# Moving the filling no-operations on TensorE in a fused retention and feed-forward kernel

## The chip, the core and the metric

The kernel runs on one core of a Trainium2 chip. The metric is the device time of one execution in microseconds (us). The engines of the core are named as in the profile: PE is TensorE (matmuls), PEld its weight loads, DVE is VectorE, ACT is ScalarE, POOL is GpSimd, SP is SyncE, which issues most transfers. Each engine has a sequencer that takes the engine's instructions from a stream in order. A no-operation is an instruction that only the sequencer handles.

## The reference

Retention over 8 batches, 8 heads, 576 positions and a head size of 64, and then a feed-forward layer with a squared ReLU over all 4608 tokens:

```python
scores = (q @ k.transpose(0, 1, 3, 2)) / np.sqrt(64)
gamma = 1.0 - 2.0 ** (-5.0 - np.arange(8))
rel = pos[:, None] - pos[None, :]
Dmat = np.where(rel >= 0, gamma[:, None, None] ** rel, 0.0)
attn = (scores * Dmat) @ v                      # [8, 8, 576, 64]
x = attn.transpose(0, 2, 1, 3).reshape(4608, 512)
r = np.maximum(x @ w_in, 0.0)                   # w_in: 512 x 2048
out = (r * r) @ w_out                           # w_out: 2048 x 512
```

All inputs and the output are float32; the kernel multiplies in float16 and sums in float32.

## The kernel before

The 4608 tokens are cut into 36 units of 128, and these into 18 groups of two. For each group the kernel loads q, k and v, casts them to float16 and brings q and k into transposed form (for the first eight units by matmuls with an identity, line 581, output psT; copies at line 598 make kqT of it). The retention of a group is made of small matmuls on quarters of the 128 x 128 array. They are all issued by one helper, at line 499: scores (psc), sums of the running state (psS) and outputs (psO). From group 4 on, the outputs of one group and the scores and sums of the next are issued as one task, a long run of 96 to 128 small matmuls, each with its own weight load, so of 194 to 258 instructions. Two TensorE instructions stand for each matmul in the stream, a weight load and the matmul.

The feed-forward layer takes x of a group (xT) through w_in (line 1226, output ph), ReLU and square on ScalarE and VectorE, and w_out (line 1267 for group 0, line 1324 after that, output po). From group 1 on, the second product is done by Strassen's scheme with seven products of half the size in place of eight (sums gS on VectorE, line 1297). Groups 13 to 16 do the first product in the same way (line 1069). Before the change and after it this is the same.

The program is written out by a planner, `Schedule`. A kernel's piece of work is a task with an engine, a modelled duration `dur`, tasks that it depends on, and a `size`, roughly its number of TensorE instructions. `emit` plays the tasks through a model of the engines, with a key for each task from the table PLACES, and so gets one order for all of them. Then it calls `place_runs` with TensorE's tasks in this order. `place_runs` writes into tasks a number `pad`; and when the program is at last written out, each task's instructions are followed by `pad` no-operations on TensorE (`sched.filler`, line 393). No other engine gets any.

Warm-up matmuls (line 408, 34 of them, tasks with keys of 10^6 at first and `size=2`) multiply zeros at the start. The first 15 have a modelled duration of 0.43 us, the very first one of 1.75.

In the kernel before, `place_runs` counts instructions and gives each long run (`size` over 200) a place within blocks of 256 instructions: where the run's place isn't between 60 and 196 behind an assumed edge, it spreads as many no-operations as bring it to 130 over the tasks since the last task of a size over 20. Three runs get some: 136, 125 and 128, in all 389.

Of the kernel before, what the change touches and what calls it, by code (L numbers as in the profile page):

```python
# [78 lines left out]
class Schedule:  # L79
# [118 lines left out]
            for i in range(t["pad"]):  # L198
                self.filler()

    BLOCK, EDGE, AHEAD_OF, SAFE = 256, 194, 130, (60, 196)

    def place_runs(self, tasks):

        at = 3
        between = []
        for t in tasks:
            if t["size"] > 200:
                phase = (at - self.EDGE) % self.BLOCK
                if not self.SAFE[0] <= phase <= self.SAFE[1]:  # L210
                    n = (self.AHEAD_OF - phase) % self.BLOCK
                    for i, x in enumerate(between):
                        x["pad"] += n * (i + 1) // len(between) - n * i // len(between)
                    at += n
            at += t["size"]
            if t["size"] > 20:
                between = []
            else:
                between.append(t)


# [1246 lines left out]
```

## Time and profile before

| what | value |
|---|---|
| three runs | 285.14, 285.28, 286.89 us |
| median | 285.28 us |
| profiled execution | 285.75 us |
| its span, first to last instruction | 284.0 us |
| instructions in the profile, all engines | 10,985 |
| no-operations at line 393 | 389 |
| granted TensorE clock, mean of the span | 1.000 |
| bytes moved | 50.00 MB, 176 GB/s on average |

A row of a timeline gives the start in us from the span's start, the length, the engine, the line, the operation, output and inputs by the program's names, the shape and the count; in brackets the idle time before and what ended it. A matmul's modelled length covers its way through the pipeline, so that rows overlap; the distance of two starts tells what one costs. A row of the chain of work that ended last gives start, length and what the time was spent on; "issue" in it is time in which an engine waited for nothing that the profile shows.

### The profile page before, as it was taken

The numbers are of one execution on the slowest core, as the hardware profiler recorded it, in microseconds if no ns is written. First come the engines' busy times: TensorE is split into PE (matmuls) and PEld (weight loads), VectorE is DVE, ScalarE is ACT, GpSimd is POOL, SyncE is SP. The second block draws the span as 40 slices with busy tenths as digits, with TensorE's granted clock in tenths as the row PEclk, the third lists the DMA queues.
The fourth block names the chain that finished last, engine by engine and source line by source line (L and its number), as shares of the span: only waits on it lengthen the run. The fifth ranks groups of instructions, "written<-read, shape, count | busy, mean of one in ns | idle before, by whom it ended". The sixth has DMA issues, their size and how long they took to land.

```text
span 284.0 us, 10985 instructions
## 1 busy us (share of the span) xinstructions
PE 277.2 (98%) x4538; PEld 236.1 (83%) x4538; DVE 196.3 (69%) x380; ACT 191.8 (68%) x357; POOL 85.4 (30%) x123
## 2 busy tenths in 40 slices
PE   8899999999999999999999999999999999999994
PEld 3577767887888888888888888898899999999983
DVE  4783589755777856746648668687798799874562
ACT  5659984678485856885577685757739585867830
POOL 6650036424334441524342523425141500000000
PEclk9999999999999999999999999999999999999999
DMA  7999999989799899999889888979997921120114
GB/s 211 288 207 207 263 312 239 178 224 162 175 193 211 161 218 193 199 248 193 202 210 213 191 175 198 163 171 223 172 208 177 179 95 39 39 76 2 39 38 148
DMA packets 119152, 50.00 MB, mean 176 GB/s; under 512 B 94784, under 2 KB 113728, under 8 KB 119104
## 3 DMA queue, kind: packets, MB, share of 16 engines
q1 hardware_dynamic: 114560, 44.84, 71.5%
q0 software_dynamic: 4224, 4.19, 8.9%
q8 instruction: 37, 0.61, 0.9%
q10 hardware_dynamic: 320, 0.26, 0.4%
q14 instruction: 11, 0.09, 0.1%
HBM read 36.70 MB, written 9.44 MB: 162 GB/s over the span
## 4 chain that ended last, share of the span: by engine, by line
PE 93%; POOL 2%; issue 2%; DVE 1%; ACT 1%; POOLq 0%; DVEq 0%
PE po L1324 37%; PE ph L1226 33%; PE ph L1069 9%; PE psO L499 5%; PE po L1267 2%; PE psS L499 2%; PE psc L499 2%; PE warm L408 1%; PE psT L581 1%; DVE gS L1297 1%; POOL mask L348 1%; ACT rl L1234 0%; POOL vx L559 0%; POOL w_in L475 0%; DVE o L1347 0%
## 5 line engine op out<-in xcount | busy, mean ns | idle before, releaser
L1226 PE MATMUL ph<-xT,w_in 128*128 128x256 f16 x896 | 108.0, 273 | 0.0
L1226 PEld LDWEIGHTS <-w_in 128*128 128x128 f16 x896 | 86.5, 98 | 11.8 <-issue 0.5
L1234 ACT ACTIVATE rl<-ph 128x512 f16<-128x512 f32 x112 | 65.5, 589 | 27.3 <-PE ph L1226 26.3
L1244 ACT ACTIVATE gT<-rl 128x512 f16<-128x512 f16 x94 | 59.0, 630 | 2.5
L1324 PEld LDWEIGHTS <-gS 128*128 128x128 f16 x544 | 51.3, 98 | 7.3 <-issue 0.6
L1324 PE MATMUL po<-wT,gS 128*128 128x256 f16 x408 | 55.2, 273 | 0.1
L1324 PEld LDWEIGHTS <-gT 128*128 128x128 f16 x408 | 38.6, 98 | 5.7 <-issue 0.6
L1324 PE MATMUL po<-w_out,gT 128*128 128x256 f16 x272 | 37.4, 273 | 0.0
L1297 DVE TENSOR_TENSOR gS<-gT,gS 128x512 f16<-128x512 f16 (+1 forms) x51 | 31.0, 614 | 9.3 <-ACT gT L1244 8.7
L529 POOL TENSOR_TENSOR v<-loads,vdec_full 128x512 f16<-128x512 f32 x24 | 27.0, 1125 | 29.1 <-DMA loads<-in_v_dram 13.9
L513 POOL CAST kq<-loads 128x512 f16<-128x512 f32 x32 | 21.8, 682 | 35.0 <-DMA loads<-in_k_dram 26.0
L1297 DVE TENSOR_TENSOR gS<-gT 128x1024 f16<-128x1024 f16 x34 | 27.0, 796 | 6.9 <-ACT gT L1244 5.8
L524 POOL CAST kq<-loads 128x512 f16<-128x512 f32 x24 | 15.6, 649 | 43.7 <-DMA loads<-in_q_dram 43.5
L1347 DVE TENSOR_TENSOR o<-po,u 128x256 f32<-128x256 f32 x33 | 13.9, 421 | 20.2 <-PE po L1324 15.8
L1337 ACT COPY u<-po 128x256 f32<-128x256 f32 x34 | 12.6, 370 | 18.9 <-PE po L1324 18.9
L895 DVE TENSOR_TENSOR xT<-psO,gam_full 128x512 f16<-128x512 f32 x28 | 18.5, 684 | 6.0 <-PE psO L499 5.9
L1103 DVE CUSTOM_DVE_ANT_0 gT<-ph,loads 128x512 f16<-128x512 f32 x24 | 16.0, 687 | 6.2 <-PE ph L1069 4.0
L1082 ACT COPY loads<-ph 128x512 f32<-128x512 f32 x24 | 13.7, 586 | 9.4 <-PE ph L1069 8.9
L1324 PE MATMUL po<-wT,gT 128*128 128x256 f16 x136 | 19.3, 273 | 0.0
L1324 PE MATMUL po<-w_out,gS 128*128 128x256 f16 x136 | 18.2, 273 | 0.0
L1117 ACT ACTIVATE gT<-gT 128x1024 f16<-128x1024 f16 x16 | 16.4, 1054 | 0.3
L835 DVE TENSOR_TENSOR rT<-psc,mask_full 128x512 f16<-128x512 f32 x24 | 16.0, 682 | 0.7 <-PE psc L499 0.7
(101 smaller groups left out, 324.8 us busy)
## 6 DMA issues: line engine op xcount, KB each, us to landing
out_dram<-o SPq DMA_DIRECT2D x32, 256.0 KB, 2.9
loads<-in_k_dram SPq DMA_DIRECT2D x24, 256.0 KB, 4.6
loads<-in_q_dram SPq DMA_DIRECT2D x96, 64.0 KB, 3.6
loads<-in_v_dram SPq DMA_DIRECT2D x24, 256.0 KB, 3.4
w_in<-in_moe_w_in_dram POOLq DMA_DIRECT2D x4, 512.0 KB, 9.1
w_out<-in_moe_w_out_dram POOLq DMA_DIRECT2D x4, 512.0 KB, 14.3
pair_c<-in_k_dram SPq DMA_DIRECT2D x2, 512.0 KB, 5.6
pair_c<-in_q_dram SPq DMA_DIRECT2D x4, 256.0 KB, 5.8
```

The costliest lines, as they stand in the source:

```text
L499: t = nc.tensor.matmul(out_, lhsT=lhsT, rhs=rhs, start=start, stop=True, skip_group_check=True, tile_position=(64 * row, 64 * col))
L513: op(out=out_.rearrange("p (n b a d) -> p n b a d", n=2, b=2, a=2), in_=in_.rearrange("p (a n b) d -> p n b a d", n=2, a=2))
L529: nc.gpsimd.tensor_tensor(out=t, in0=tile_of["v32", u], in1=vdec[kind].rearrange("p (h o) -> p h o", o=1).to_broadcast([P, H, D]), op=ALU. ...
L835: tile_of["masking", g] = nc.vector.tensor_tensor(out=tile_of["rT", g][:, :, a], in0=tile_of["psc", g][a].rearrange("p (s n i) -> p s n i" ...
L895: nc.vector.tensor_tensor(out=tile_of["x", g].rearrange("p n (s e i) -> p e (n s) i", s=n, e=2)[:, c], in0=y.rearrange("p (o t r) -> p o r ...
L1069: nc.tensor.matmul(out_[:, e], lhsT=left[:, m, fi * P:(fi + 1) * P], rhs=right()[:, m], start=fresh and e == 0 and m == 0, stop=m == HK - ...
L1117: nc.scalar.activation(out=t, in_=t, func=ACTF.Square)
L1226: nc.tensor.matmul(tile_of["ph", g, fb][:, j, :], lhsT=w_in16[:, m, fi * P:(fi + 1) * P], rhs=tile_of["x", g][:, m, :], start=(m == 0), st ...
L1234: nc.scalar.activation(out=t, in_=tile_of["ph", g, fb], func=ACTF.Relu)
L1244: nc.scalar.activation(out=t, in_=rl, func=ACTF.Square)
L1297: (nc.gpsimd if eng == "POOL" else nc.vector).tensor_tensor(out=tile_of["S", g][:, k, sl], in0=in0(sl), in1=in1(sl), op=op)
L1324: nc.tensor.matmul(tile_of["pb", g, bank], lhsT=left(i), rhs=right[:, i, :], start=(start and i == 0), stop=(i == HF - 1), skip_group_chec ...
```

## The change

`place_runs` no longer counts places in blocks. It takes the number of no-operations for each place from a list. The first number, 139, goes to the first 15 warm-up matmuls. The others go ahead of the runs of a `size` over 190, in order, over the tasks of `size` up to 8 that begin later than 24 us in the planner's model and stand since the last such run. Within a place they are spread in proportion to the tasks' modelled durations. The order of the tasks, and so of every other instruction, stays as it was.

```diff
-    BLOCK, EDGE, AHEAD_OF, SAFE = 256, 194, 130, (60, 196)
+    WARM, PADS = 15, (139, 34, 22, 4, 2, 66, 56, 44, 62, 2, 2, 10, 66)
 
     def place_runs(self, tasks):
 
-        at = 3
+        def spread(n, among):
+            total = sum(x["dur"] for x in among)
+            until, done = 0.0, 0
+            for x in among:
+                until += x["dur"]
+                upto = int(n * until / total + 1e-6)
+                x["pad"] += upto - done
+                done = upto
+
+        pads = iter(self.PADS)
+        spread(next(pads), [t for t in tasks if t["key"] >= 10 ** 6 and t["size"] == 2][:self.WARM])
         between = []
         for t in tasks:
-            if t["size"] > 200:
-                phase = (at - self.EDGE) % self.BLOCK
-                if not self.SAFE[0] <= phase <= self.SAFE[1]:
-                    n = (self.AHEAD_OF - phase) % self.BLOCK
-                    for i, x in enumerate(between):
-                        x["pad"] += n * (i + 1) // len(between) - n * i // len(between)
-                    at += n
-            at += t["size"]
-            if t["size"] > 20:
+            if t["size"] > 190:
+                spread(next(pads, 0), between or [t])
                 between = []
-            else:
+            elif t["size"] <= 8 and t["key"] < 10 ** 6 and t["start"] > 24.0:
                 between.append(t)
```

In the written program TensorE's stream grows from 9,505 to 9,625 instructions, no-operations from 389 to 509: 31 behind the first warm-up matmul, 7 or 8 behind each of the next 14, and 370 in the twelve other places.

## The prediction

> **What bounds the kernel now.** I read the first part of the page, then the chain that ended last, then TensorE's timeline, and last the records of the no-operations. Of the page:
>
> ```profile
> PE 277.2 (98%) x4538; PEld 236.1 (83%) x4538; DVE 196.3 (69%) x380; ACT 191.8 (68%) x357; POOL 85.4 (30%) x123
> PE 93%; POOL 2%; issue 2%; DVE 1%; ACT 1%; POOLq 0%; DVEq 0%
> q8 instruction: 37, 0.61, 0.9%
> ```
>
> TensorE works through 98% of the span and is 93% of the chain, so whatever makes its stream longer makes the kernel longer. The third line counts the packets of 16,384 bytes (0.61 MB in 37) that bring TensorE's own instructions; 256 instructions of 64 bytes fill one, and 37 of them make 9,472 of the stream's 9,505. No packet lies before 14.6 us.
>
> The start, from TensorE's timeline (start, length, line, operation, output and inputs, count, idle time before and its releaser):
>
> ```profile
> 5.07 0.98 PE L408 MATMUL warm<-wT 128*128 128x512 f16 x3
> 5.88 0.74 PE L581 MATMUL psT<-ident,kx 128*128 128x128 f16 x8
> 6.46 0.81 PE L408 MATMUL warm<-wT 128*128 128x512 f16 x3
> 7.10 0.71 PE L581 MATMUL psT<-ident,qx 128*128 128x128 f16 x8
> 7.65 1.46 PE L408 MATMUL warm<-wT 128*128 128x512 f16 x6
> 9.73 0.64 PE L499 MATMUL psc<-kqT 64*64 64x128 f16 x31 [0.46 <-DVE kqT L598]
> 10.70 0.45 PE L499 MATMUL psS<-vx,kx 64*64 64x64 f16 x32 [0.33 <-POOL vx L559]
> 16.51 0.70 PE L499 MATMUL psS<-vx,kx 64*64 64x64 f16 x32
> ```
>
> From 10.70 us on, TensorE hardly waits again. Until then GpSimd's vx (ready at 10.65) sets the pace, and TensorE's two idle spells (0.46 and 0.33) are all the slack that it has there.
>
> The no-operations cost TensorE's sequencer time. Between 66.8 and 68.06 us, by the view of line 393:
>
> ```profile
> L393 PEldq NOP  x16: 13/13/13, 66.8 to 68.0; - x16
> ```
>
> Their records start 71 ns apart (66.835, 66.905, 66.976, 67.047), and the same 1.26 us holds eight matmuls of 109 ns, 0.87 us of work. So four no-operations to two matmuls take some 0.315 us instead of 0.218. At most 1.26/16 = 79 ns go to one, pairs of weight load and matmul included; a pair by itself issues in about 20 ns. In the chain (start, length, what):
>
> ```profile
> 65.65 2.50 PE po L1324 x20
> 70.98 1.10 PE po L1324 x8
> 129.81 2.40 PE po L1324 x22
> 223.33 0.29 issue
> ```
>
> 20 x 109 ns is 2.18, 8 x 109 ns is 0.87: dense no-operations cost 0.32 and 0.23 us here. The 22 matmuls at 129.81 have about one no-operation each and take just 22 x 109 ns: at one each they are free. The "issue" at 223.33 is idle time that nothing in the profile ended.
>
> **The change part by part.** The order of TensorE's other 9,116 instructions and their waits stay; so do the instructions of all other engines and every DMA. 389 no-operations leave three places (136 among 96 matmuls before the run of small matmuls at 72.97, 125 among 166 before 132.14, 128 among 96 before 157.71). 509 come: 139 among the first 15 warm-up matmuls (31 behind the first, 7 or 8 behind each other), 370 over the twelve stretches from 24 us on.
>
> Step 1, warm-ups, to the first transposes. 12 warm-ups precede the transposes of kx, and 115 no-operations stand among these. 115 x 71 ns + 12 x 20 ns = 8.4 us from the first matmul at 1.25, so the transposes start at 9.7 instead of 5.88. They have no slack: the timeline shows no idle time before them, and VectorE's two casts of kx run from 5.13 to 6.16. A cold warm-up takes 0.43 us (nine in 1.25 to 5.07), less than 8 x 71 = 0.57, so TensorE itself hides none of the excess; without the 0.43 the price would be the same, as the sequencer is the later of the two.
>
> Step 2, from there to psS. Three more warm-ups with 24 no-operations: 24 x 71 + 3 x 20 ns = 1.8 us, so qx is transposed from 11.6 (7.10 before) to 12.2. The copies to kqT then take ScalarE and VectorE 0.6 to 0.7 us, until 12.95; six warm-ups (1.29 us, no no-operation among them) end later, at 13.4. psc's 32 matmuls (0.57 us in their second run) follow, and psS starts at about 14.1 instead of 10.70, with vx long there: **+3.4 us**. With 79 ns for a no-operation it is +4.5; for the lower end I let the slack swallow 0.4 more, +3.0. Behind psS nothing gives this back: GpSimd's w_in transfers wait for a load, not for TensorE, and the next casts sit on ScalarE with 0.8 us or more to spare.
>
> Step 3, dense no-operations removed. The chain's pieces with four to a pair of matmuls lose 0.32 (65.65), 0.09 (68.15), 0.05 (69.54), 0.08 (70.46), 0.23 (70.98), 0.09 (72.08) and 0.08 (155.90): **-0.94 us**; -0.7 to -1.1 by how the 109 ns is rounded. What replaces them is at most 66 among 166 or 62 among 116 matmuls, 0.4 to 0.55 each, and the 125 among 166 were free: cost nothing, hidden beside 109 ns matmuls. Were that cover gone, 62 would cost 4.4 us; no row suggests it.
>
> Step 4, waits for instructions. Counting TensorE's stream, its instruction 451 (195 + 256) stands in the psS at 16.51, which took 0.70 where its twin at 10.70 took 0.45; instruction 7,875 (195 + 30 x 256) stands at the gap at 223.33. So blocks begin at 195 + 256n, and both stalls are a block not yet there. The second: block edge 7,619 was passed 0.25 us into the run of small matmuls at 219.60, the packet for the block after next came at 221.32, took 0.93, and work went on at 223.6, 3.7 us behind the passing. Afterwards 7,619 lies 60 instructions ahead of that run, which are 25 matmuls or 2.7 us, and the next edge 196 into it, 1 us: 3.7 us, plus what the sequencer is ahead of TensorE (packets that start up to 1.7 us before their edge is executed show such a lead). The stall should vanish: -0.45 (the gap in matmul starts is 0.51 against 0.056). Edge 451 falls in the later psO, 6.3 us behind edge 195; the first packet needed 6.0 the last time: -0.24. Together **-0.69**, between -0.69 and +0.5 if a stall of this size appears elsewhere; I take -0.69, as the shortest other distance of two edges is 4.35 us. Small pauses inside the runs (0.07 to 0.2 us, some 0.8 in all) have edges inside the same runs as before: 0, from -0.4 to +0.4.
>
> [...]
>
> **Sum.** The profiled execution took 285.75 us: span 284.0 and 1.75 around it. 285.75 + 3.4 - 0.94 - 0.69 = 287.5. The median shown is 285.28, 0.47 below that execution, so on its scale the forecast is **287.0 us**, +0.6%. Its own range, from 3.0 and the full gains (1.1 + 0.69 + 0.4) to 4.5 and the small ones (0.7 - 0.5 - 0.4): 286.1 to 290.0 at the extremes (0.4 of the small pauses in both), 286.4 to 288.0 in the main.
>
> **Rivals.**
>
> The no-operations are hidden (faster): if one costs under about 40 ns at the start, 115 fit into the 4.6 us before 5.88, and only steps 3 and 4 remain: 285.28 - 1.63 = 283.65. For it: warm-ups have the sequencer idle 0.4 us each. Against it: the 71 ns stand in the records without exception, and are no shorter where the sequencer had nothing else to do.
>
> The clock opens late (slower still). The page's granted clock is full in every slice, but warm-up matmuls of 512 columns stand 427 ns apart until about 5.4 us, 4.1 after the first, and 216 ns apart from there: the array gets its full rate only then. After the change it is idle for 1.8 us behind the first matmul, then busy 0.43 in each 0.53 to 0.59 us. If the clock stays at half to psS, three warm-ups and eight transposes take 2.1 instead of 1.8 us (+0.3), the second transposes 0.4 more, six warm-ups 2.6 instead of 1.3, psc some 0.3 more: +2.3, 289.3. [...] The rows show it opening after 4.1 us of unbroken work, and nothing with less; I think that 75% will mostly do.
>
> The stalls do not go (the change doesn't do what it says): step 4 gives 0 or +0.5, and the sum is 287.7 to 288.2.
>
> **How the numbers follow.** Forecast 0.64, late clock 0.18, stalls stay 0.08, hidden 0.10. The range is 284.8 to 289.6: it leaves out the hidden case and the far ends of the late clock and of the forecast. A measurement of this kernel tells about 1% from no change: slower by more (over 288.13) is the late clock, half of the stalls and the top of the forecast, 0.28; faster by more (under 282.43) is beyond even the hidden case, 0.04; within 1%, 0.68.
>
> **What would show it.** kx's transposes at 9.7 and psS at 14.1 us (steps 1, 2); everything from there 3.2 us late; 20 matmuls in 2.18 us where 65.65 stands (3); no "issue" piece near the feed-forward matmuls behind the run at 219.60 (4); the clock's rise by the length of a warm-up matmul. I am wrong if the no-operations at the start lie closer than 71 ns, or if a later wait of TensorE shrinks by what the start lost.

## The result, and the profile after

| | before | after |
|---|---|---|
| median of 22 runs each, us | 286.16 (285.14 to 290.52) | 287.80 (286.60 to 289.44) |
| profiled execution, us | 285.75 | 288.55 |
| its span, us | 284.0 | 286.8 |

The ratio after to before is 1.0046, with a 95% interval of 1.0026 to 1.0067. The changed kernel is a little slower, by an amount that lies below the 1% that a measurement of this kernel tells from no change with few runs, and that 22 runs on each side resolve. It is the ratio of the means, 287.80 and 286.47 us, without the one slow execution of the kernel before, 290.52 us; by the medians the difference is 1.64 us, by these means 1.33. The forecast was 287.0 us, +0.6%.

Lines have moved by 4: 408 is 412 now, 581 is 585, 499 is 503, 1324 is 1328, 393 is 397. The first part of the page, the chain's shares and the instruction packets, for the changed kernel:

```profile
PE 279.0 (97%) x4538; PEld 237.5 (83%) x4538; DVE 195.3 (68%) x380; ACT 191.6 (67%) x357; POOL 87.5 (31%) x123
PE 97%; issue 1%; DVE 1%; DVEq 0%
q8 instruction: 37, 0.61, 0.9%
```

TensorE still sets the end. GpSimd has gone from the chain: before, the chain's first microseconds ran through GpSimd and its vx; now TensorE itself is late there. The start, from TensorE's timeline of the changed kernel (start, length, engine, line, operation, output and inputs, shape, count, idle time before and its releaser):

```profile
1.25 0.61 PE L412 MATMUL warm<-wT 128*128 128x512 f16 x1 [1.25 <-DVE wT L293]
3.54 6.39 PE L412 MATMUL warm<-wT 128*128 128x512 f16 x11 [1.68 <-issue]
9.87 1.01 PE L585 MATMUL psT<-ident,kx 128*128 128x128 f16 x8
10.68 1.49 PE L412 MATMUL warm<-wT 128*128 128x512 f16 x3
11.96 1.06 PE L585 MATMUL psT<-ident,qx 128*128 128x128 f16 x8
12.81 1.86 PE L412 MATMUL warm<-wT 128*128 128x512 f16 x6
15.07 0.42 PE L503 MATMUL psS<-vx,kx 64*64 64x64 f16 x32
20.86 0.44 PE L503 MATMUL psS<-vx,kx 64*64 64x64 f16 x32
```

The 31 no-operations behind the first warm-up matmul are the pause of 1.68 us. The transposes of kx start at 9.87, where they stood at 5.88, and psS at 15.07 instead of 10.70. The second psS takes 0.44 us, where it took 0.70: the wait inside it is gone. The lengths tell one thing more. Before, three warm-ups took 0.98 us in the row at 5.07 and 0.81 in the one at 6.46, and eight transposes 0.74; here they take 1.49 and 1.01, and the six warm-ups 1.86 instead of 1.46. Where no no-operations stand between them, a warm-up stands 427 ns from the next until 13.6 us, and 216 ns from there on. 216 ns is the array's full rate here, and it came only at 13.6 us, 8.2 later than before (5.4). The page's row of granted clock has a 9 (90% or more) in every slice here as before, so what sets the moment isn't shown; where the recorded texts say that the clock opens, the traces show this step from 427 to 216 ns.

Further on, pieces of the chain (start, length, what; 20 matmuls of 109 ns are 2.18 us, 8 are 0.87):

```profile
69.71 2.18 PE po L1328 x20
74.51 0.87 PE po L1328 x8
133.40 2.40 PE po L1328 x22
223.66 0.46 issue
```

The dense no-operations have gone: 2.18 us where 2.50 stood at 65.65, 0.87 where 1.10 stood at 70.98. But an "issue" piece still stands behind the run at 219.60 of before (now at 222.6). It has moved from the feed-forward matmuls into the run of small ones, and the distance of matmul starts there is 0.65 us too long. In TensorE's stream it is the same place as before, instruction 7,875.

The time can be booked by comparing the start of each matmul with the start of the same matmul before. The same booking was made for three more executions of the unaltered changed kernel (they come up again below):

| how much later than before (us), at | after | 1st again | 2nd again | 3rd again | forecast |
|---|---|---|---|---|---|
| psS (10.70 before) | 4.37 | 3.79 | 4.08 | 4.01 | 3.4 |
| behind the stall at 451 (16.93) | 4.11 | 3.57 | 3.86 | 3.80 | 3.16 |
| behind the dense stretch (72.01) | 3.21 | 2.85 | 2.96 | 2.90 | 2.30 |
| 199.69 | 2.98 | 2.65 | 2.21 | 1.94 | 2.22 |
| behind instruction 7,875 (223.62) | 2.89 | 2.02 | 2.01 | 1.53 | 1.77 |

The last row is what is left at the end. Its mean is 2.11 us, and 285.75 + 2.11 is 287.86, the median of the 22 runs within 0.1. The profiled execution of the table is the latest of the four.

### The profile page after: what moved, and what is told of

Same layout as the page of the kernel before. It is cut to its first block, busy times and chain, and to the rows that moved or that the text cites. A ratio compares the mean times of both kernels' runs of the same rounds, so it can differ in the third digit from the quotient of the medians.

```text
span 286.8 us, 11105 instructions
## 1 busy us (share of the span) xinstructions
PE 279.0 (97%) x4538; PEld 237.5 (83%) x4538; DVE 195.3 (68%) x380; ACT 191.6 (67%) x357; POOL 87.5 (31%) x123
## 4 chain that ended last, share of the span: by engine, by line
PE 97%; issue 1%; DVE 1%; DVEq 0%
PE po L1328 37%; PE ph L1230 34%; PE ph L1073 9%; PE psO L503 5%; PE warm L412 5%; PE po L1271 2%; PE psc L503 2%; PE psS L503 2%; PE psT L585 2%; DVE o L1351 0%; DVE p L1380 0%; DVE wT L293 0%; DVEq L1351 0%
## 5 line engine op out<-in xcount | busy, mean ns | idle before, releaser
L517 POOL CAST kq<-loads 128x512 f16<-128x512 f32 x32 | 21.2, 661 | 35.9 <-DMA loads<-in_k_dram 25.9
L1301 DVE TENSOR_TENSOR gS<-gT 128x1024 f16<-128x1024 f16 x34 | 24.1, 710 | 8.9 <-ACT gT L1248 7.8
L528 POOL CAST kq<-loads 128x512 f16<-128x512 f32 x24 | 16.8, 701 | 33.0 <-DMA loads<-in_q_dram 32.9
L1341 ACT COPY u<-po 128x256 f32<-128x256 f32 x34 | 12.6, 370 | 18.5 <-PE po L1328 18.5
L1250 DVE TENSOR_TENSOR gT<-rl 128x512 f16<-128x512 f16 x18 | 9.7, 541 | 14.2 <-ACT rl L1238 14.0
L412 PE MATMUL warm<-wT 128*128 128x512 f16 x34 | 14.1, 490 | 3.0 <-issue 1.7
```

The source lines that it names most:

```text
L412: nc.tensor.matmul(warm_ps[0], lhsT=junk[:, 0:P], rhs=junk, start=True, stop=True)
L517: op(out=out_.rearrange("p (n b a d) -> p n b a d", n=2, b=2, a=2), in_=in_.rearrange("p (a n b) d -> p n b a d", n=2, a=2))
L528: nc.gpsimd.tensor_copy(out=tile_of["kq", u][:, 1].rearrange("p (t a d) -> p a t d", t=4, a=2), in_=tile_of["q32", u].rearrange("p (a t) d ...
L1301: (nc.gpsimd if eng == "POOL" else nc.vector).tensor_tensor(out=tile_of["S", g][:, k, sl], in0=in0(sl), in1=in1(sl), op=op)
```

## The experiments

**No no-operations among the warm-ups.** The 139 move to the next place (34 + 139 = 173), so that every later instruction keeps its number in the stream.

```diff
-    WARM, PADS = 15, (139, 34, 22, 4, 2, 66, 56, 44, 62, 2, 2, 10, 66)
+    WARM, PADS = 15, (0, 173, 22, 4, 2, 66, 56, 44, 62, 2, 2, 10, 66)
```

> The changed kernel without any no-operation among the warm-up matmuls: the 139 go to the next place instead (173 in place of 34, among 258 matmuls from 24 us on), so that every long run keeps its instruction numbers. Theory of the sequencer's time: the transposes of kx are back at 5.9 us and psS at 10.7 (15.1 in the changed kernel), the 0.24 us stall of instruction 451 comes back, and 173 among 258 matmuls cost nothing: 4.1 us less than the changed kernel, about 283.7 where that has 287.8 and the kernel before 286.2. Rival, that the no-operations at the start are free or are paid back later and the changed kernel is slower for another reason (stalls at other block edges): no difference from the changed kernel, 287.8.

Measured: 284.13 us (8 runs) against 285.82 for the kernel before (13 runs on the same chip), ratio 0.9944 (0.9926 to 0.9963). From its timeline:

```profile
1.26 4.75 PE L412 MATMUL warm<-wT 128*128 128x512 f16 x12 [1.26 <-DVE wT L293]
5.84 0.61 PE L585 MATMUL psT<-ident,kx 128*128 128x128 f16 x8
10.76 0.45 PE L503 MATMUL psS<-vx,kx 64*64 64x64 f16 x32 [0.32 <-POOL vx L563]
16.57 0.38 PE L503 MATMUL psS<-vx,kx 64*64 64x64 f16 x22
17.18 0.28 PE L503 MATMUL psS<-vx,kx 64*64 64x64 f16 x10 [0.24 <-issue]
```

The start is that of the kernel before again: transposes at 5.84, psS at 10.76 behind vx, and the stall at instruction 451 is back. The 173 no-operations ahead of the first long run cost nothing that shows (the 20 matmuls behind 65.86 take 2.18 us). So what is slow in the change is the 139 at the start, and the other 370 make the kernel faster than before. Its profile also has a pause of 0.46 us at instruction 5,315, and none at 7,875.

**The no-operations at the start alone.** The kernel before, with its first 136 no-operations moved from the stretch ahead of the first long run to the first 15 warm-ups; the other two places stay.

```diff
+        first = next(i for i, t in enumerate(tasks) if t["size"] > 200)
+        n = sum(t["pad"] for t in tasks[:first])
+        for t in tasks[:first]:
+            t["pad"] = 0
+        among = [t for t in tasks if t["key"] >= 10 ** 6 and t["size"] == 2][:15]
+        total = sum(x["dur"] for x in among)
+        until, done = 0.0, 0
+        for x in among:
+            until += x["dur"]
+            upto = int(n * until / total + 1e-6)
+            x["pad"] += upto - done
+            done = upto
```

> The kernel before with one part of the change alone: its first 136 no-operations leave the 96 matmuls ahead of the run at 72.97 us and stand among the first 15 warm-up matmuls. Theory of the sequencer's time: psS at about 15 us instead of 10.70 (+4.3), instruction 451 no longer stalls (-0.24), and the dense stretch gives back 0.9: about +3.2, 289.4 where the kernel before has 286.2. Rival, no-operations at the start are free: only the 0.9 and 0.24 remain, 285.0.

Measured: 287.70 us (4 runs), ratio 1.0074 (1.0054 to 1.0093). From its timeline:

```profile
3.47 6.21 PE L420 MATMUL warm<-wT 128*128 128x512 f16 x11 [1.61 <-issue]
9.75 0.61 PE L593 MATMUL psT<-ident,kx 128*128 128x128 f16 x8
11.53 0.61 PE L593 MATMUL psT<-ident,qx 128*128 128x128 f16 x8 [0.24 <-issue]
11.98 1.46 PE L420 MATMUL warm<-wT 128*128 128x512 f16 x6
13.96 0.46 PE L511 MATMUL psS<-vx,kx 64*64 64x64 f16 x32
```

psS is 3.26 us late, the stall at 451 gives back 0.22 and the dense stretch 0.87; 2.18 us are left at 72.01 of before, and 1.96 at the end. That the start costs nothing is refuted (285.0 was its time). The 289.4 expected, with a late full rate in it, was too high: the full rate came at 9.5 us, ahead of the transposes, eight of which take 0.61 us. The stall at 7,875 stands in this kernel too, 0.90 us by the matmuls' starts, where the kernel before had 0.45 with the same stream behind 73 us: such a stall isn't the same in two executions.

**A denser array under the same no-operations.** Each of the first 15 warm-ups issues its matmul twice, so that the array is busy while the sequencer passes the no-operations. This adds 15 matmuls of zeros whose result nobody reads; 30 no-operations are taken from the next place to keep the later places in the stream.

```diff
-    WARM, PADS = 15, (139, 34, 22, 4, 2, 66, 56, 44, 62, 2, 2, 10, 66)
+    WARM, PADS = 15, (139, 4, 22, 4, 2, 66, 56, 44, 62, 2, 2, 10, 66)
...
-        nc.tensor.matmul(warm_ps[0], lhsT=junk[:, 0:P], rhs=junk, start=True, stop=True)
+        made.append(1)
+        for i in range(2 if len(made) <= 15 else 1):
+            nc.tensor.matmul(warm_ps[0], lhsT=junk[:, 0:P], rhs=junk, start=True, stop=True)
```

> The changed kernel with two matmuls in place of one in each of the first 15 warm-ups, so that the array stays busy between the no-operations (30 no-operations fewer in the next place keep the long runs' instruction numbers). Theory that the thinned warm-up opened the clock late (13.6 us in the changed kernel, 5.4 before): it opens before 9 us, the 24 no-operations ahead of the transposes of qx set the pace and psS comes at 14.1 instead of 15.07: 0.9 less, about 286.9 where the changed kernel has 287.8. Rival, that the clock opens when it will whatever stands there: 13.6 again, psS at 15.1 or a little later, 287.8 or 0.3 more.

Measured: 287.39 us (6 runs), ratio 1.0052 (1.0033 to 1.0071). From its timeline:

```profile
3.54 6.58 PE L414 MATMUL warm<-wT 128*128 128x512 f16 x22 [1.25 <-issue]
9.96 0.61 PE L588 MATMUL psT<-ident,kx 128*128 128x128 f16 x8
14.30 0.46 PE L506 MATMUL psS<-vx,kx 64*64 64x64 f16 x32
```

The full rate came at 6.97 us, and the transposes take 0.61 us where the changed kernel's first ones take 1.01. psS stands at 14.30, +3.6 with a full rate that comes ahead of the transposes; 3.4 was forecast for the no-operations alone, and three more warm-ups stand ahead of qx's transposes here. (Its profiled execution is the shortest of the six, 286.46 us: 3.6 us behind the kernel before at psS, and 0.77 at the end.) In the times, a gain of 0.4 to 0.8 us over the changed kernel can't be seen (ratios 1.0052 and 1.0046 to the kernel before, with intervals of 0.2% on each side). So the start's cost is chiefly the sequencer's, and the late full rate is a part that only the profile shows.

**Half of them.** 70 among the warm-ups, and the other 69 in the next place.

```diff
-    WARM, PADS = 15, (139, 34, 22, 4, 2, 66, 56, 44, 62, 2, 2, 10, 66)
+    WARM, PADS = 15, (70, 103, 22, 4, 2, 66, 56, 44, 62, 2, 2, 10, 66)
```

> The changed kernel with 70 no-operations among the first 15 warm-ups in place of 139 (15 behind the first, 3 or 4 behind each other), 69 more in the next place, so that the long runs keep their instruction numbers. Theory of the sequencer's time: 4 x 71 + 20 ns = 0.30 us is less than the 0.43 us of a warm-up at the half clock, so only the 15 behind the first delay TensorE (0.7 us), and the slack of 0.8 us ahead of psS takes that: psS within 0.5 us of 10.7, the time that of the kernel with none there (284.1) to 0.5 more. Rival, that each no-operation costs its 71 ns in any place: half of the 4.0 us between none and 139, 286.1.

Measured: 284.66 us (10 runs) against 286.29 (23 runs on the same chip), ratio 0.9936 (0.9912 to 0.9960). From its timeline:

```profile
2.36 3.85 PE L412 MATMUL warm<-wT 128*128 128x512 f16 x11 [0.49 <-issue]
6.05 0.61 PE L585 MATMUL psT<-ident,kx 128*128 128x128 f16 x8
11.27 0.45 PE L503 MATMUL psS<-vx,kx 64*64 64x64 f16 x32 [0.32 <-POOL vx L563]
```

Half of the no-operations don't cost half of 4 us: the time is that of the kernel without any at the start (ratios 0.9936 and 0.9944 to the kernel before). Three or four behind a warm-up (0.21 to 0.28 us) are less than the 0.43 us that its matmul lasts at half rate; only the 15 or so behind the first make a pause, 0.49 us, and psS still waits for GpSimd's vx, as it did before (vx itself came 0.6 us later in this execution, which the end doesn't show; in the two experiments below that have no no-operation at the start it came 0.5 us later too, so it isn't these that delay it). Seven or eight (0.50 to 0.57 us) are more than 0.43: in the changed kernel the warm-ups that they follow start 0.52 to 0.62 us apart. So the cost doesn't grow in proportion: 70 show none in the time, and 139 a psS that is 3.79 to 4.37 us late.

**More distance at 7,875.** The last place gets 126 no-operations instead of 66, so that the edge 7,619 lies 120 instructions ahead of the run of small matmuls in place of 60, and the edge 7,875 falls 135 instructions into the run in place of 196.

```diff
-    WARM, PADS = 15, (139, 34, 22, 4, 2, 66, 56, 44, 62, 2, 2, 10, 66)
+    WARM, PADS = 15, (139, 34, 22, 4, 2, 66, 56, 44, 62, 2, 2, 10, 126)
```

> The changed kernel with 60 more no-operations in its last place (126 in place of 66, among 178 matmuls), so that block edge 7,619 lies 120 instructions ahead of the run at 222.5 us in place of 60. Theory that the 0.65 us pause inside this run (instruction 7,875, 223.47 us) is a block that hasn't come 3.7 us after the edge before it was passed: the distance grows by 2.7 us, the pause goes, 0.6 less: about 287.2 where the changed kernel has 287.8; 0.7 no-operations to a matmul cost nothing. Rival, that the run itself waits there for VectorE or for an earlier matmul: the pause stays at the same small matmul, 287.8 or, with no-operations that cost, more.

Measured: 288.46 us (4 runs), ratio 1.0094 (1.0073 to 1.0116), where a gain on the changed kernel was expected. From its chain:

```profile
207.99 3.22 PE po L1328 x22
217.52 1.69 PE po L1328 x14
219.67 1.43 PE ph L1073 x24
223.66 0.52 PE psO L503 x48
```

The pause at 7,875 is gone (no "issue" piece; the 48 psO follow each other). But 22 matmuls take 3.22 us where the kernel before has 2.51 at 206.11, and in all the matmuls between 206.7 and 216.4 us of before lose 1.2 us. The tasks that take no-operations there (`size` up to 8) are few and hold pairs of matmuls, so that the 126 come out, in places, as three and four behind two matmuls; four to a pair is the density that cost 0.32 on 20 matmuls in the kernel before. The expectation had counted them as hidden.

**Both at once: the start without, more distance, and more tasks to spread over.**

```diff
-    WARM, PADS = 15, (139, 34, 22, 4, 2, 66, 56, 44, 62, 2, 2, 10, 66)
+    WARM, PADS = 15, (0, 173, 22, 4, 2, 66, 56, 44, 62, 2, 2, 10, 126)
...
-            elif t["size"] <= 8 and t["key"] < 10 ** 6 and t["start"] > 24.0:
+            elif t["size"] <= 16 and t["key"] < 10 ** 6 and t["start"] > 24.0:
```

> The kernel with no no-operation among the warm-ups (173 in the first of the later places) and two more edits: the last place gets 126 in place of 66, so that block edge 7,619 lies 120 instructions ahead of its run, and the no-operations are spread over tasks of size up to 16 in place of 8, so that the 16 matmul products of line 1069 take their share and none of them stand in fours behind two matmuls. Theory: the pause at instruction 7,875 (0.65 us) goes, the 1.2 us that the denser 126 cost at 209 to 220 us are not paid: 0.6 less than 284.1, 283.5, some 0.8% under the kernel before. Rival, that 126 cost there however they are spread: 284.1 or more.

Measured: 285.18 us (12 runs), ratio 0.9953 (0.9928 to 0.9978): no gain on the first experiment, and 0.5% under the kernel before where 0.8% was expected. Both parts of the theory hold in the trace: from 206.7 to 216.4 us of before the 126 cost nothing (TensorE is 1.27 us late at both ends), and of the pause at 7,875 only 0.11 us are left. But other waits stand in this execution: 0.90 us at instruction 2,755, 0.32 at 5,315, and 0.89 for VectorE's sum gS. At 286.36 us it is also the second slowest of the twelve, so that it says less of the median. Pieces of its chain, at instruction 2,755, where none of the other kernels with this numbering stalls:

```profile
86.39 0.22 PE psS L503 x19
86.61 0.71 issue
87.31 0.29 PE psS L503 x13
```

The packet of that stretch started at 84.11 us, 4.5 us behind the edge that it belongs to, where the six before it started 0.6 to 3.0 us behind theirs. It took 1.6 us until 85.7, and work went on at 87.3. The distance from the edge before was 6.8 us here, without the pause, far more than the 3.7 on which the prediction built. So a long distance doesn't exclude a stall, and the first experiment passed 7,875 without one at the changed kernel's own distance.

**None at all.** Every no-operation is left out.

```diff
-    WARM, PADS = 15, (139, 34, 22, 4, 2, 66, 56, 44, 62, 2, 2, 10, 66)
+    WARM, PADS = 15, (0,)
```

> The changed kernel with no no-operation at all, to see what they are for. Block edges then lie at 6, 30, 3, 25 and 39 instructions into five of the long runs, with the next edge 4 to 37 instructions behind the run's end, and 63 ahead of one more. If a block comes 3.7 us or more behind the edge that asks for it, these runs stall by 0.5 to 2.5 us each, some 5 to 8 us together, and the time is 288 to 291. Rival, that fetching is mostly hidden: no stall, and nothing lost to no-operations, 283.5.

Measured: 290.09 us (4 runs), ratio 1.0109 (1.0056 to 1.0162). From its chain:

```profile
158.38 1.82 issue
175.59 0.91 issue
195.17 0.57 issue
```

The waits stand at instructions 5,059, 5,571 and 6,339, all of the form 195 + 256n, and are 1.89, 1.07 and 0.76 us long by the distance of matmul starts; a fourth of 0.31 stands at 6,851. Each comes in or behind a run of small matmuls, at 8 ns or so to a matmul and its weight load, with which TensorE takes the block before it in 1.2 to 3.3 us; with the wait included, edge and edge are 3.1 to 4.0 us apart in all four. By the ratios to the kernel before (1.0109 and 0.9944) the no-operations of the first experiment are worth 1.65%, 4.7 us. That they are idle ballast is refuted. Of the 35 crossings of this kernel these four cost 4.0 us together, in the shortest of the four executions (287.96 us).

**The changed kernel again, three executions.** Nothing is altered.

> The changed kernel unaltered, for what differs between executions of one program. Theory that the clock's opening and the arrival of an instruction block vary by execution: the clock opens somewhere from 7 to 14 us, psS comes at 13.9 to 15.1 accordingly, and the pauses at instructions 5,315 and 7,875 are anywhere from 0 to 0.7 us. Rival, that the program fixes them: 13.6, 15.07, 0.31 and 0.65 us again.

> As for the first repetition: opening from 7 to 14 us and pauses of 0 to 0.7 us if they vary by execution; 13.6 us, 0.31 and 0.65 us if the program fixes them.

> As for the first repetition: opening from 7 to 14 us and pauses of 0 to 0.7 us if they vary by execution; 13.6 us, 0.31 and 0.65 us if the program fixes them.

Measured: 287.70, 287.69 and 287.21 us, beside 286.29 for the kernel before. From the timelines, of the first:

```profile
9.86 1.01 PE L585 MATMUL psT<-ident,kx 128*128 128x128 f16 x8
11.95 0.72 PE L585 MATMUL psT<-ident,qx 128*128 128x128 f16 x8
12.50 1.46 PE L412 MATMUL warm<-wT 128*128 128x512 f16 x6
14.49 0.46 PE L503 MATMUL psS<-vx,kx 64*64 64x64 f16 x32
```

and of the second:

```profile
9.86 1.01 PE L585 MATMUL psT<-ident,kx 128*128 128x128 f16 x8
11.95 1.01 PE L585 MATMUL psT<-ident,qx 128*128 128x128 f16 x8
12.79 1.46 PE L412 MATMUL warm<-wT 128*128 128x512 f16 x6
14.78 0.46 PE L503 MATMUL psS<-vx,kx 64*64 64x64 f16 x32
```

To the transposes of kx the executions agree within 0.01 us: that part is the sequencer's. From there they differ by when the full rate comes. With the kernel that has 126 no-operations in the last place, whose start is the same instructions, there are five executions of one start:

| full rate from (us) | psS starts at (us) |
|---|---|
| 11.0 | 14.15 |
| 12.2 | 14.49 |
| 12.6 | 14.71 |
| 12.8 | 14.78 |
| 13.6 | 15.07 |

Each microsecond by which the full rate is later costs about 0.35 us (0.92 over 2.6). The pause at 7,875 is 0.65, 0.10, 0.38 and 0 us in the four executions of the changed kernel, and the one at 5,315 is 0.31, 0.31, 0 and 0. So neither belongs to the placing alone; that they vary by execution holds, within the bounds expected, and the rival, that the program fixes them, is refuted.

What a pause at an edge follows can be read from the twelve traces, with the instruction packets counted in order beside the edges 195 + 256n. A packet starts anywhere from 1.8 us ahead of its edge to 5.6 us behind it, and takes 0.9 to 2.3 us. In all 17 pauses of 0.19 us or more at an edge (one more stands among dense no-operations), work goes on 1.2 to 1.6 us after the end of the packet that belongs to the edge before. At every other of the some 400 crossings that packet had ended at least 1.3 us earlier. So the wait is one for instructions, and the distance of two edges decides it only together with the moment at which the packet starts. At 5,315, for instance, the edges are 5.9 us apart; the packet started 3.4 to 3.6 us behind the edge before in the four executions of this numbering that pause there, and 0.8 to 3.1 us in the five that don't. Why a packet starts late is open.

## Why the prediction was right, point by point

The forecast of 287.0 on the scale of the runs, +1.7 us, stands against 287.80 and +1.64 by the medians, +1.33 by the means of the ratio; the range of 284.8 to 289.6 holds it. Part of the nearness is luck, two errors that cancel, as the steps show.

**Step 1, right.** kx's transposes were to start at 9.7 and start at 9.86 or 9.87 in five executions. 115 no-operations at 71 ns, with the sequencer as the later of the two, give the number; the "half" kernel shows the other side, where the array is the later one (0.21 to 0.28 us of no-operations beside a matmul of 0.43).

**Step 2, under-sized, by a part that was put in a rival.** psS was to start at 14.1, +3.4, and started at 14.15 to 15.07; in the four executions of the changed kernel +4.06 on average, 0.66 more than forecast. The sentence that failed is "I think that 75% will mostly do". The array came to its full rate at 11.0 to 13.6 us, 7 to 10 us behind the second warm-up, although warm-ups kept it busy some three quarters of that time (0.43 in each 0.52 to 0.62 us ahead of kx's transposes). The rival had the late full rate, but priced it to the extreme, with half rate up to psS (+2.3). The full rate comes ahead of psS in all five, and the excess over 14.1 is 0.05 to 0.97. The kernel with doubled warm-ups tells the two parts from each other: full rate at 6.97, psS still at 14.30. With the unbroken start the full rate came at 5.3 to 5.5 us, 4.1 to 4.2 behind the first matmul; with the thinned one of the changed kernel three quarters didn't do. Why they didn't, and why the moment differs between executions of one program, no run shows.

**Step 3, right.** -0.94 was forecast; the dense stretch gives -0.90, -0.72, -0.90 and -0.90 where -0.86 belonged, and the piece near 156 about -0.1. The no-operations that replace them cost nothing that the chain shows: 22 matmuls take 2.40 at 133.40, 20 take 2.18 at 156.18. The cover of 109 ns matmuls held at one no-operation to a matmul or less, as step 3 had it, and gave way in the kernel with 126, as the prediction's clause on that cover has it.

**Step 4, right in the first half, half right in the second.** The stall at instruction 451 goes, -0.21 to -0.26 against -0.24. But it varies by execution as well: the four kernels that start without no-operations (before, the first experiment, both at once, none at all) wait 0.23, 0.43, 0 and 0 us there. At 7,875, -0.45 was forecast for certain; between 199.69 and 223.62 us the executions give -0.09, -0.63, -0.20 and -0.41, -0.33 on average. The distance there was mis-sized: the prediction has 7,619 and 7,875 3.7 us apart after the change, and they are 3.1 apart without the pause, less than the 3.3 of the kernel before, for 14 of the 60 instructions ahead of the run are no-operations beside 23 matmuls, which pass in 2.3 us and not in 2.7. The step's premise was that a block arrives 3.7 us behind the passing of the edge, a constant from one stall of one execution. The kernel before itself has the edges 3,523 and 3,779 3.2 us apart without a pause; the packet started 1.2 us ahead of the first. The runs show a spread in place of the constant: at the pauses, packets start 0.6 to 4.5 us behind the edge and take 0.9 to 1.6 us, and waits of 0 to 0.65 us come at one place in one program. So the gain at 7,875 didn't come from a longer distance.

**Not in the forecast: a gain between 72 and 200 us.** -0.08 was due there (the no-operations at 155.90), and the four executions give -0.23, -0.20, -0.75 and -0.96. 0.32 to 0.34 of it is seen in all four between 185.38 and 199.69: before, TensorE waited 0.29 us at 199.3 for the sum gS of VectorE, a piece of the chain of the kernel before:

```profile
197.47 2.17 DVE gS L1297 x2
```

In the changed kernel this wait is gone. In the first two executions a new pause of 0.31 at instruction 5,315 takes it back. That "a later wait of TensorE shrinks by what the start lost" stood among what would make the prediction wrong, and a later TensorE would find its inputs readier. But lateness isn't shown to be the cause: the first experiment, whose TensorE is 0.7 us early at 185.38, gains the same 0.33 us there, and with TensorE nearly on time the wait for gS came too (0.46 us by its matmul starts in the kernel with half the no-operations, 0.89 in the combined one). The rest, up to 0.6 in the third repetition, is small pauses, whose single causes stay open.

The mean of the four adds up to 4.06 - 0.23 - 0.86 - 0.53 - 0.33 = 2.11 us, against 3.4 - 0.24 - 0.86 - 0.08 - 0.45 = 1.77: the start was forecast 0.66 too cheap, and the stretch from 72 us 0.33 too dear. On the scale of the profiled execution that makes 287.86 against the forecast's 287.5. That the forecast subtracted 0.47 to get to the median of three runs was a step too far: over 22 runs the kernel before has a median of 286.16, and 285.75 is below most of them.

**The rivals.** The no-operations hidden (283.65): refuted at 139 by the transposes at 9.87. With 70 they are hidden, not because one costs less (none lies closer than 70 ns to the next there either) but because the matmul beside them lasts longer (0.43 us against 0.21 to 0.28). The clock late (289.3): the late full rate came, at 0.05 to 0.97 us of its +2.3. The stalls do not go (287.7 to 288.2): true of the executions with a pause at 7,875, and the measured time lies among these; but the first stall went, and the profiles put the excess at the start.

## What to carry to other kernels

A no-operation on TensorE cost its sequencer 71 ns here. Three or four behind a warm-up (0.21 to 0.28 us beside 0.43) cost nothing that the time shows, seven or eight (0.50 to 0.57) were part of a start that came 3.79 to 4.37 us later, so a number that is free at half of its size can cost microseconds at full size. The fillers of the first experiment were worth 4.7 us of 290: without any, TensorE waited 0.31 to 1.89 us at four edges 195 + 256n, in or behind runs of tiny matmuls. In this kernel they belong beside long matmuls behind the start (173 of them ahead of the first long run cost nothing that shows), not among the warm-ups. The kernel with the first number at 0 (or 70) is the one to keep: 0.6% under the kernel before, 1.0% under the changed one.

## What the runs showed of the hardware

The array came to its full rate at 5.3 to 5.5 us behind unbroken warm-ups, at 5.1 with half of the no-operations, at 6.97 with doubled warm-ups, and at 9.5 and 11.0 to 13.6 behind thinned ones; one program differs by 1.4 us between its own executions (12.2 to 13.6). The page's row of granted clock has a 9 in every slice before and after; only the distance of matmul starts (427 against 216 ns) tells it.

The waits at instruction edges vary as well. One program stalls at a given edge (7,875) for 0, 0.10, 0.38 and 0.65 us, and a packet that has landed doesn't end the wait at once: in 17 pauses, 1.2 to 1.6 us went by from its end to the next matmul.
